# A decode layer on one core: three unused matmuls between the wide rows of w_down and the fold

## The chip, the cores and the metric

The kernel runs on one core of a Trainium2 chip. The metric is the device time of one execution in microseconds. Three runs of the kernel before took 409.50, 410.06 and 410.45 us; the median is 410.06. The engines are called TensorE (PE in the views, PEld for its weight loads), VectorE (DVE), ScalarE (ACT), GpSimd (POOL) and SyncE (SP, which issues the DMAs).

## What is computed

One token goes through a transformer layer with a cache of 65,536 positions. All inputs are bf16.

```python
def _A_ref(x, k_cache, v_cache, wq, wo):      # 32 query heads, 4 cache heads, head size 128
    q = (x @ wq).reshape(B, Sq, Hq, Dh).transpose(0, 2, 1, 3)
    k = jnp.repeat(k_cache, rep, axis=1)
    v = jnp.repeat(v_cache, rep, axis=1)
    p = _softmax(jnp.einsum("bhqd,bhkd->bhqk", q, k) * (Dh ** -0.5), axis=-1)
    o = jnp.einsum("bhqk,bhkd->bhqd", p, v)
    return o.transpose(0, 2, 1, 3).reshape(B, Sq, Hq * Dh) @ wo

def _B_ref(x, w_gate, w_up, w_down):          # 1024 -> 3584 -> 1024
    return (_gelu(x @ w_gate) * (x @ w_up)) @ w_down

h  = A_x + _A_ref(_layernorm(A_x), A_k_cache, A_v_cache, A_wq, A_wo)
h2 = h + _B_ref(_layernorm(h), B_w_gate, B_w_up, B_w_down)
```

## The kernel before

The two caches and the five weight matrices are read once, 173 MB in all, through one DMA queue that SyncE issues. A ring of four slots in SBUF takes wq, then the caches in eight turns (four cache heads, two halves each), then wo, w_gate, w_up and most of w_down. Because there is one token, every matmul has the weights or the cache as its moving operand. Its result is one useful row, and the kernel places four such narrow matmuls, 32 columns of the array each, side by side (`tile_position`).

The attention part is a list of operations with waits worked out by the class `Flow`, and a hardware loop of eight turns on TensorE (`pe_loop`). Its scores come from L464: 128x512 bf16 moving, 128x128 weights out of the tile `qs`. After the loop the tile `qs` and PSUM bank 5 are not used any more.

The feed-forward part is a plain program, in which TensorE's instructions stay in the order in which they are written (`manual_schedule`). w_down comes in four main loads, in this order: `wa` (4096 KB, the first 16 rows of each partition), `wb[:, 0:FM]` (2048 KB, 8 rows), `w_end[:, 0:3]` (768 KB, 3 rows) and the first five eighths of a last row (160 KB). The rest of that last row comes ahead of them in small pieces (L685 uses them). TensorE waits for each load on a semaphore of its own (`end_sem`).

The end of the kernel, in TensorE's order:

- L646 multiplies by w_up, L679 and L685 deal with the odd part of the last row.
- L665 (`down_wide`) multiplies the 16 rows of `wa`, two matmuls of 512 columns for each row, into bank 6 (`e_ps`), summing at four places of 32 partitions.
- L690 is ScalarE's copy of bank 6 to SBUF (`e_sb`), 128x512 f32.
- L671 (`add_wide`, the fold) adds the four places and brings them into the layout of the result: four f32 matmuls with the constant weights `fold`, two instructions each, into banks 2 and 7 (`d_ps`, `d_odd`).
- L657 (`down`) multiplies the other rows of w_down straight into those two banks, eight matmuls of 128 columns for each row: 64 for `wb`, 24 for the three rows in `w_end` and 5 for the last one, 93 in all.
- L699 and L700 cast the two banks to bf16, on VectorE and ScalarE, and L701 stores the result.

The fold reads what the copy writes, so TensorE waits for it between L665 and L671.

Of the kernel before, what the change touches and what calls it, by code (L numbers as in the profile page):

```python
# [118 lines left out]
def kernel(  # L119
# [13 lines left out]
    nc = tc.nc  # L133
    P = 128
# [21 lines left out]
    NB = 512  # L156
# [25 lines left out]
    def sb(name, shape, dtype=F32):  # L182
        return const.tile(shape, dtype, name=name)
# [3 lines left out]
    qs = sb("qs", [P, 4, NS, P + 1], BF16)  # L187
    sc = sb("sc", [P, CPH, NN, rep, NS])
    pt = sb("pt", [P, CPH, NN, rep, NS], BF16)
    bank = [psum.tile([P, NB], F32, name="bank%d" % i) for i in range(8)]  # L190
# [172 lines left out]
    for q in range(4):  # L363
        op("pe", "matmul", r=["q_bf"] + ["esel"], w=["B5"], out=qsel_ps[:, :, q, :], lhsT=esel[:, q, :], rhs=q_bf[:],
           start=True, stop=True)
# [156 lines left out]
    for dq in range(OQ):  # L522
        op("pe", "matmul", r=["o_sb", "osel"], w=["B4"], out=o2_ps, lhsT=osel[:, dq, :], rhs=o_sb[:, dq * Hq:(dq + 1) * Hq],
           start=(dq == 0), stop=(dq == OQ - 1))
# [17 lines left out]
    for c in range(Hq):  # L542
        for s in range(DS):
            q = 2 * (c % 2) + s
            op("pe", "matmul", r=["o2z", "R%d" % (2 + c // HC)], w=["B6"], out=at_ps[32 * q:32 * q + 32, :], lhsT=o2z[:, c, :],
               rhs=wv[:, c, :].rearrange("k (p s c) -> k s p c", s=DS, c=C4)[:, s], start=(c < 2), stop=(c >= Hq - 2), tile_position=(0, 32 * q))
# [104 lines left out]
    def down(a_row, w_row):  # L651
        blocks = w_row.shape[-1] // OB
        for j in (0, 4, 1, 5, 2, 6, 3, 7):
            if j >= blocks:
# [2 lines left out]
            nc.tensor.matmul((d_ps, d_odd)[q // 2][32 * q:32 * q + 32, :], lhsT=a_row[:, AZ - m:AZ - m + 32], rhs=w_row[:, j * OB:(j + 1) * OB],  # L657
                             start=False, stop=False, skip_group_check=True, tile_position=(0, 32 * q))

    e_sb = sb("e_sb", [P, NB])  # L660

    def down_wide(a_row, w_row, e):
        for h in range(DS):
            q = 2 * (e % 2) + h
            nc.tensor.matmul(e_ps[32 * q:32 * q + 32, :], lhsT=a_row[:, AZ:AZ + 32], rhs=w_row[:, h * NB:(h + 1) * NB],  # L665
                             start=False, stop=False, skip_group_check=True, tile_position=(0, 32 * q))

    def add_wide():
        for c in range(C4):
            h = c % 2  # L670
            nc.tensor.matmul((d_ps, d_odd)[h][64 * h:64 * h + 64, :], lhsT=fold[:, 1 - c // 2:65 - c // 2], rhs=e_sb[:, c * OB:(c + 1) * OB],  # L671
                             start=False, stop=False, skip_group_check=True, tile_position=(0, 64 * h))
# [9 lines left out]
    for s in range(GS + 1):  # L682
        q = 2 * (s % 2) + 1
        n = min(GN, P - s * GN)
# [3 lines left out]
    for e in range(FA):  # L688
        down_wide(actz[:, e, :], wa[:, e, :], e)
    nc.scalar.copy(out=e_sb[:], in_=e_ps[:])  # L690
    add_wide()
    e = FA
    for i, w_rows in ((2, wb[:, 0:FM, :]), (3, w_end[:, 0:FZ - 1, :]), (4, w_end[:, FZ - 1:FZ, 0:EC])):
# [38 lines left out]
```

## Time and profile before

| | |
|---|---|
| median of three runs | 410.06 us |
| the profiled execution: its time | 409.35 us |
| the profiled execution: its span, first to last instruction | 407.63 us |
| mean granted TensorE clock over the span | 0.803 |
| HBM read | 173.02 MB, 424 GB/s over the span |
| copy L690 | 400.57 to 401.16 us |
| fold L671 | 401.21 to 402.34 us |
| L657, 64 and 29 matmuls | 402.31 to 404.20 and 404.16 to 405.06 us |
| cast L699 | from 405.09 us |
| store L701 issued | 405.45 us |

Times inside the execution count from the first instruction of the span. A matmul's record goes from its start to a modelled end; matmuls overlap, so the distance between starts says how fast they follow one another. The granted clock is the share of full speed at which TensorE's array ran; in the records it is 1.0 or 0.5 and changes on a grid of 3.41 us, so a stretch with 0.59 is a mixture of the two. A DMA is complete when all its 16 parts have landed. "Idle before" is the time for which an engine had nothing running ahead of an instruction, with what ended it.

### The profile page before, as it was taken

What the parts mean: (1) busy time and instruction counts of PE and PEld (TensorE: products, weight loads), DVE (VectorE), ACT (ScalarE), POOL (GpSimd) and SP (SyncE); (2) the same over time, 40 slices, a digit from 0 to 9 for tenths busy, and PEclk for the clock granted to TensorE, in tenths of its full rate; (3) what the DMA queues carried; (4) which work ended last, traced back from release to release, by engine and by line L of the source; (5) the groups of instructions that cost most, each with busy time, mean ns of one, the idle gap of its engine ahead of it and who ended that gap; (6) DMA issues with size and microseconds to landing.
All of it is one profiled execution on the core that took longest, in us unless ns stands there. A gap on an engine that the chain in (4) does not pass through costs nothing. (4 is left out here: it accounts for less than half of the span.)

```text
span 407.6 us, 3801 instructions
## 1 busy us (share of the span) xinstructions
PE 226.5 (56%) x1546; PEld 99.3 (24%) x1546; DVE 201.4 (49%) x164; ACT 40.2 (10%) x143; POOL 14.6 (4%) x27
## 2 busy tenths in 40 slices
PE   0432854674677468716873686368456637634056
PEld 0110322231232133203321332133122213222023
DVE  4126860894079328734962686188509930111110
ACT  1000003000300130030003000300040022000000
POOL 4010000001000000010000001000000000001100
PEclk9995896899569778968896689589968986566686
DMA  8999999999999999999998999999999999999995
GB/s 360 412 453 420 447 428 412 460 419 431 434 460 418 412 441 479 418 408 415 495 424 386 441 421 453 415 463 412 412 460 460 418 408 424 457 450 424 405 410 222
DMA packets 5105, 173.10 MB, mean 425 GB/s; under 512 B 616, under 2 KB 876, under 8 KB 1004
## 3 DMA queue, kind: packets, MB, share of 16 engines
q1 hardware_dynamic: 5052, 173.02, 98.6%
q8 instruction: 4, 0.07, 0.1%
q10 hardware_dynamic: 48, 0.00, 0.0%
q14 instruction: 1, 0.01, 0.0%
HBM read 173.02 MB, written 0.00 MB: 424 GB/s over the span
## 5 line engine op out<-in xcount | busy, mean ns | idle before, releaser
L105 DVE STREAM_TRANSPOSE ktb<-ring 128x4096 f32<-128x4096 f32 x32 | 141.1, 4417 | 74.7 <-DMA ring<-in_A_k_cache_dram 74.7
L464 PE MATMUL bank<-ktb,qs 128*128 128x512 bf16 x512 | 130.0, 412 | 53.4 <-PEq L450 53.4
L464 PEld LDWEIGHTS bank<-ktb,qs 128*128 128x128 bf16 x512 | 50.9, 102 | 129.2 <-issue 82.1
L476 PE MATMUL bank<-ring,pt 128*32 128x512 bf16 x512 | 44.4, 522 | 38.0 <-PEq L450 38.0
L423 ACT ACTIVATE pt<-sc,nb 128x256 bf16<-128x256 f32 x64 | 31.5, 494 | 256.3 <-ACTq L419 256.3
L105 DVE STREAM_TRANSPOSE sc<-bank 128x512 f32<-128x512 f32 x32 | 22.2, 695 | 36.3 <-PE bank L464 36.3
L476 PEld LDWEIGHTS bank<-ring,pt 128*32 128x32 bf16 x512 | 18.5, 126 | 60.7 <-issue 56.7
L105 PE MATMUL bank<-ring,xz 128*32 128x512 bf16 (+1 forms) x128 | 11.9, 546 | 15.1 <-DMA ring<-in_B_w_gate_dram 8.2
L105 DVE TENSOR_REDUCE mx<-sc 128x8 f32<-128x2048 f32 x8 | 18.3, 2286 | 0.3
L468 PE MATMUL bank<-ident_f,mx 128*8 128x128 f32 x8 | 2.5, 308 | 25.8 <-PEq L450 25.8
L105 POOL COPY qs<-qsel 128x512 bf16<-128x512 bf16 x4 | 5.3, 1324 | 235.4 <-PE bank L464 219.8
L485 PE MATMUL bank<-sel,acc_sb 128*128 128x8 f32 x64 | 8.2, 255 | 6.9 <-PEq L450 6.9
L423 ACT ACTIVATION_READ_ACCUMULATOR pt<-sc,nb x64 | 12.0, 187 | 0.0
L485 PEld LDWEIGHTS bank<-sel,acc_sb 128*128 128x128 f32 x64 | 7.7, 191 | 10.7 <-issue 10.7
L646 PE MATMUL bank<-ring,xz 128*32 128x512 bf16 (+1 forms) x64 | 4.6, 457 | 9.3 <-PEq L641 9.3
L105 PEld LDWEIGHTS bank<-ring,xz 128*32 128x32 bf16 x128 | 4.4, 129 | 21.5 <-issue 12.7
L427 ACT COPY acc_sb<-bank 128x512 f32<-128x512 f32 x8 | 4.7, 585 | 47.9 <-ACTq L426 47.9
L623 DVE STREAM_TRANSPOSE ktb<-bank 128x512 f32<-128x512 f32 (+1 forms) x4 | 2.3, 618 | 13.3 <-PE bank L646 13.3
L105 PE MATMUL bank<-ring,ktb 128*32 128x512 bf16 x64 | 7.1, 618 | 1.7 <-DMA ring<-in_A_wo_dram 1.0
L468 PEld LDWEIGHTS bank<-ident_f,mx 128*8 128x8 f32 x8 | 0.7, 83 | 29.5 <-issue 29.5
L105 DVE STREAM_TRANSPOSE ktb<-bank 128x512 f32<-128x512 f32 x2 | 1.3, 694 | 12.6 <-PE bank L105 12.6
L470 PE MATMUL bank<-diag,ones_f 8*128 8x8 f32 x16 | 3.5, 286 | 5.7 <-PEq L450 5.7
(110 smaller groups left out, 65.7 us busy)
## 6 DMA issues: line engine op xcount, KB each, us to landing
ring<-in_A_k_cache_dram SPq DMA_DIRECT2D x16, 4096.0 KB, 24.8
ring<-in_A_wq_dram SPq DMA_DIRECT2D x2, 4096.0 KB, 16.6
ring<-in_A_wo_dram SPq DMA_DIRECT2D x2, 4096.0 KB, 25.4
ring<-in_B_w_gate_dram SPq DMA_DIRECT2D x1, 7168.0 KB, 24.6
ring<-in_B_w_up_dram SPq DMA_DIRECT2D x1, 7168.0 KB, 30.3
ring<-in_B_w_down_dram SPq DMA_DIRECT2D x1, 4096.0 KB, 17.5
ring<-in_B_w_down_dram SPq DMA_DIRECT2D x1, 2048.0 KB, 22.0
w_end<-in_B_w_down_dram SPq DMA_DIRECT2D x1, 768.0 KB, 23.4
```

The costliest lines, as they stand in the source:

```text
L105: ins = getattr(self.eng[e], o["call"])(**o["kw"])
L423: m = nc.scalar.activation(out=pt[:].rearrange("p c n h s -> p (c n) h s")[:, :, r, :], in_=sc[:].rearrange("p c n h s -> p (c n) h s")[:, ...
L427: nc.scalar.copy(out=acc_sb[:], in_=acc[:]).then_inc(from_act, 1)
L464: m = nc.tensor.matmul(bank[c][:], lhsT=qs[:, jt].rearrange("p s c -> p (s c)")[:, s * P:(s + 1) * P], rhs=mv[:, :, J, :, u], start=(s == ...
L468: nc.tensor.transpose(out=mxT_ps, in_=mx1[:], identity=ident_f).then_inc(s_step, 1)
L470: nc.tensor.matmul(bc_ps, lhsT=ones_f[0:rep, :], rhs=diag[:], start=True, stop=True).then_inc(s_step, 1)
L476: m = nc.tensor.matmul(acc[32 * q:32 * q + 32, :], lhsT=pt[:, c, n, :, :].rearrange("p h s -> p (h s)"), rhs=v_sb[:, c, :, n, :], start=(c ...
L485: m = nc.tensor.matmul(o_ps, lhsT=acc_sb[:, u * Dh:(u + 1) * Dh], rhs=sel[:, u:SQ:NS], start=(u == 0), stop=(u == NS - 1))
L623: nc.vector.transpose(out=r[:, o:o + n].rearrange("p (e j) -> p e j", j=32), in_=ps.rearrange("p (j e) -> p e j", j=32))
L646: nc.tensor.matmul(f_banks[t // 4][32 * q:32 * q + 32, :], lhsT=hz[:, ci, :], rhs=w, start=(ci == 0), stop=(ci == DC - 1), tile_position=( ...
```

## The change

Between the last wide row and the fold, three matmuls are issued. Each takes 128x128 bf16 weights and 128x512 bf16 moving data out of the old tile `qs` and writes bank 5, which nothing reads. They stand in TensorE's program behind L665 and ahead of the fold's wait for the copy, and wait for nothing of the feed-forward part. No other engine's instructions and no DMA are changed.

```diff
+    def stay_busy(n):
+        for i in range(n):
+            nc.tensor.matmul(bank[5][:], lhsT=qs[:, 0, 0, 0:P], rhs=qs[:, 1 + i % 3].rearrange("p s c -> p (s c)")[:, 0:NB], start=True, stop=True)
+
     e_sb = sb("e_sb", [P, NB])
...
     for e in range(FA):
         down_wide(actz[:, e, :], wa[:, e, :], e)
     nc.scalar.copy(out=e_sb[:], in_=e_ps[:])
+    stay_busy(3)
     add_wide()
```

## The prediction

> **What bounds the kernel now.** I read the page first, then the chain of waits, then the timeline of the last 12 us, then the DMA issues, and last the table by stages, cut on the grid of 3.41 us on which the granted clock changes. The page settles the whole: the DMA queue that carries the caches and weights is busy for 98.6% of the span, TensorE for 56%.
>
> ```profile
> PE 226.5 (56%) x1546; PEld 99.3 (24%) x1546; DVE 201.4 (49%) x164; ACT 40.2 (10%) x143; POOL 14.6 (4%) x27
> ...
> q1 hardware_dynamic: 5052, 173.02, 98.6%
> ```
>
> So only the stretch after the last big loads can give or take time. The chain of waits runs there through one transfer of w_down, the wide rows (L665), ScalarE's copy (L690), the fold (L671) and the rest of w_down (L657):
>
> ```profile
> 379.84 17.52 DMA ring<-in_B_w_down_dram
> 397.36 0.04 issue
> 397.40 3.15 PE bank L665 x32
> 400.55 0.02 issue
> 400.57 0.59 ACT e_sb L690
> 401.17 0.04 issue
> 401.21 1.12 PE bank L671 x8
> 402.34 2.77 PE bank L657 x63
> ```
>
> Read alone, it says that TensorE bounds the last 8 us and that everything queued there counts. The DMA list corrects that (columns: KB of one issue, us from issue to landing):
>
> ```profile
> ring<-in_B_w_down_dram SPq DMA_DIRECT2D x1, 2048.0 KB, 22.0
> w_end<-in_B_w_down_dram SPq DMA_DIRECT2D x1, 768.0 KB, 23.4
> w_end<-in_B_w_down_dram SPq DMA_DIRECT2D x1, 160.0 KB, 23.3
> ```
>
> With their issues just after 380.2, 380.7 and 381.2, these three land at 402.32, 404.17 and 404.57 (the last of their 16 landings in the trace). The first L657 matmul starts at 402.31: the fold's end and the landing fall together by chance. The 24 matmuls of the second load start at 404.16, again with the landing, after the first 64 had issued by 403.89. So from 402.3 on DMA sets two of three starts.
>
> The table by stages (PE busy, PEld, DVE, ACT, POOL, granted clock, DMA share, GB/s):
>
> ```profile
> 271.69:275.10 3.41, 3.41 (x9) 1.17 (x8) 3.41 (x1) 0.00 (x0) 0.00 (x0) 0.51 1.16 500
> 275.11:278.52 3.41, 3.41 (x17) 1.53 (x16) 2.31 (x3) 0.00 (x0) 0.00 (x0) 1.00 0.75 327
> ...
> 387.75:391.16 3.41, 2.87 (x32) 1.42 (x36) 0.00 (x0) 0.00 (x0) 0.00 (x0) 0.51 0.98 423
> 391.16:394.57 3.41, 1.71 (x36) 0.88 (x29) 1.64 (x4) 0.00 (x0) 0.00 (x0) 1.00 1.07 461
> 394.57:397.98 3.41, 1.89 (x24) 0.82 (x27) 0.19 (x1) 0.00 (x0) 0.00 (x0) 0.99 0.87 370
> 397.99:401.40 3.41, 2.73 (x30) 0.86 (x20) 0.00 (x0) 0.58 (x1) 0.00 (x0) 0.50 1.00 418
> 401.40:404.81 3.41, 3.41 (x99) 2.81 (x100) 0.00 (x0) 0.00 (x0) 0.00 (x0) 0.51 0.46 178
> ```
>
> Each stretch's clock follows TensorE's busy time in the stretch before it. 2.87 of 3.41 (84%) at 387.75 brought full clock at 391.16; 2.73 (80%) at 397.99 did not bring it at 401.40. Elsewhere in the span 2.79 sufficed (309.24, then 1.00) and 2.55 did not (350.20, then 0.51). The gap that keeps 397.99 to 401.40 at 80% is the 0.67 us in which TensorE waits for the copy.
>
> **The change part by part.** *Three matmuls added.* Their form, 128x512 bf16 on 128x128 weights, is that of L464, which fills the first two rows of the table: 8 weight loads in 3.41 us at half clock, 427 ns each, and 16 at full clock, 213 ns. The last four wide rows start at 399.88 to 399.90 and stream 427 ns, so the array is free at 400.31. The third filler is under way when the clock may rise at about 401.38: 400.31 + 2 x 0.427 = 401.16, 0.22 us at half clock (half of it), the other half in 0.11, free at 401.49. At half clock throughout: 400.31 + 1.28 = 401.59. The copy needs nothing of them (another bank) and ends at 401.16; the fold started at 401.21. So they delay the fold by 0.28 us, 0.38 at half clock, and by nothing (401.21 against 400.31 + 0.64) at full clock. Weight loads of 102 ns (L464) go beside the stream. There is no DMA, SP or POOL work in the edit. A wait for bank 5 or qs is long met: qs was last written at 253.7 us (POOL's fourth copy), bank 5 last read at 347.1 (the last o_raw copy). Behind them on TensorE stand the fold's 8 instructions and all 93 of L657.
>
> *Where the delay goes.* The fold's four pairs start 213 ns apart at half clock (401.48, 401.70, 401.91) and the array is free 0.81 us after its start. Delayed to 401.59 it is free at 402.40, under 0.1 us past the landing at 402.32; the 64 matmuls, 1.6 us, then stream till about 404.1, before 404.17. The two landings hide all of it; without them it would cost the whole 0.28 to 0.38.
>
> *The clock.* The fillers make the stretch to 401.40 busy nearly throughout, well over the 84% that sufficed. I take full clock from 401.4 to 404.8. The fold is then free no later than 402.30, still under the landing. L657's groups of four start 107 ns apart at half clock; the only full-clock pair of groups is the last one, 404.778 to 404.833, 55 ns. From 404.17: six groups take 0.33 us, streamed out at 404.50; then the landing at 404.57, five matmuls with the last start at about 404.64, and 0.22 us for one matmul (the 219 ns minimum at L657) end at 404.86. Before, the last ended at 405.06. Gain 0.20 us. The ends: if the narrow matmuls cannot come closer than 25 ns, the last start is 404.80 as before, and the gain 0; if the clock had risen only after the last matmul instead of at 404.8, before would have ended at 404.89 + 0.31 = 405.20, and the gain would be 0.34. I take 0.20, the row's own value: the 55 ns was measured on these matmuls.
>
> [...]
>
> *After the end.* Casts, the output's issue at 405.45 and its landing follow the last matmul at fixed distance. The sum: span 407.63 - 0.20 = 407.43. The profiled execution took 409.35, 1.72 outside its span, so 409.15; the median of the runs, 410.06, lies 0.71 above it and becomes 409.86.
>
> **Rivals.** *The clock gains nothing* (410.06, the last matmul at 405.06 as before): a gap as short as 0.67 us has no say in the clock, or the 3.41 us grid falls differently against the kernel in other runs, so that the tail has full clock already, or loses it again before the last rows. For it: the eight like turns over the cache have their half-clock stretches at different places. Against: a gap of 0.67 us leaves at most 80% of any stretch that holds it whole, and 80% did not raise the clock here. [...]
>
> *The landings do not bind in unprofiled runs* (faster). If w_down landed a microsecond sooner, TensorE would be the bound: before, the fold free at 402.02, 23 groups at 107 ns and 0.31 end at 404.8; after, fold from 401.49 free by 401.92 to 402.30, 23 x 0.0535 = 1.24 and 0.22 end at 403.4 to 403.8. That is 1.0 to 1.4 us less, 408.7 to 409.1. Against: 5 us from one landing to the next for 2 MB is the queue's 420 GB/s, the same as everywhere.
>
> *The copy is released only with the fillers* (slower). Place: L690, if its wait is met by a TensorE instruction behind the wide rows, or the fillers' writes hold up its read of PSUM. It would then start about 401.8 instead of 400.57, the fold about 402.45, a delay of 1.24 us; at half clock the last matmul ends at 402.45 + 0.81 + 23.25 x 0.107 + 0.2 = 405.95, 0.9 us late: 410.96. It decides only if the clock stays low: at full clock 402.45 + 0.43 + 0.86 = 403.74 is still ahead of the landing at 404.17, and nothing is lost. Against: before, the copy started 43 ns after the last wide row, with the fold and L657 already behind it in TensorE's program.
>
> **How the numbers follow.** Forecast 0.62 (409.86, given as 409.9); no gain 0.20; landings not binding 0.07; copy held or fillers on the path 0.11, about half of it over 0.8 us. 0.2% is 0.82 us, about what a measurement of this kernel can tell from no change; forecast and no-gain case both lie within it. With the runs' own spread (409.5 to 410.45) I put faster 0.09, same 0.82, slower 0.09. The forecast alone, with its ends of 0 to 0.34, is 409.7 to 410.1; the spread of the runs and part of the two outer rivals widen it to 409.3 to 410.6.
>
> **What would show it.** Granted clock 1.00 in the stretch from about 401.4; three matmuls of 128x512 between L665 and the fold; the fold's start 0.1 to 0.4 us behind the copy's end; L657's first start still at its landing, a wait of 0.5 us or more in front of the w_end rows, and the last matmul within 0.3 us of the last landing. Wrong if the copy starts later than 0.1 us after the wide rows, if L657's first start leaves its landing by over 0.2 us, or if the landings themselves move.

## The result and the profile after

The changed kernel takes 409.16 us (median of 19 runs, 409.09 to 409.55) against 410.06 (19 runs, 409.11 to 410.45). The ratio of the runs is 0.9985, 95% interval 0.9978 to 0.9992: about 0.6 us less, 0.3 to 0.9.

The runs say more than the medians. Of the 19 times before, 8 lie at 409.1 to 409.55 and 11 at 410.06 to 410.45, none between. Of the 19 after, all lie in the lower group. The change makes no good run better; it does away with the upper group. The execution profiled before, 409.35 us, was of the lower one. The gap between the groups is not always empty: of 62 further runs of the kernel before (those shared by the experiments below) 25 lie at 409.03 to 409.44, 22 at 409.90 to 410.41 and 15 between, at 409.52 to 409.77. What those 15 are no trace shows.

The end of the chain of waits after, up to the last cast (start, us, what):

```profile
382.19 22.10 DMA w_end<-in_B_w_down_dram
404.29 0.04 issue
404.33 0.74 PE bank L657 x29
```

The long TensorE chain from wide rows to last matmul is gone; a landing and the 29 matmuls behind it are what is left. Its timeline (start, us, engine, line, instruction; L669, L694, L675 are the wide rows, copy and fold in the changed file, L662 the unused matmuls):

```profile
397.95 3.27 PE L669 MATMUL bank<-ring,ktb 128*32 128x512 bf16 x32
...
401.16 0.82 PE L662 MATMUL bank<-qs 128*128 128x512 bf16 x3
401.28 0.58 ACT L694 COPY e_sb<-bank 128x512 f32<-128x512 f32 x1 [20.95 <-PE bank L669]
...
401.92 0.66 PE L675 MATMUL bank<-e_sb,fold 128*64 128x128 f32 x8
...
402.51 1.08 PE L657 MATMUL bank<-ring,ktb 128*32 128x128 bf16 x64
...
404.33 0.70 PE L657 MATMUL bank<-w_end,ktb 128*32 128x128 bf16 x29 [0.74 <-DMA w_end<-in_B_w_down_dram]
```

The unused matmuls run beside the copy; the fold starts 0.05 us behind the copy's end and takes 0.66 us instead of 1.12. L657's 64 matmuls take 1.08 instead of 1.90 us, and TensorE then waits 0.74 us for w_end. By the stages (PE busy, PEld, DVE, ACT, POOL, clock, DMA share, GB/s):

```profile
397.34:400.76 3.42, 3.42 (x33) 1.08 (x33) 0.00 (x0) 0.00 (x0) 0.00 (x0) 0.50 0.99 423
400.76:404.17 3.41, 2.83 (x83) 1.53 (x75) 0.00 (x0) 0.58 (x1) 0.00 (x0) 1.00 0.69 272
```

Read alone, this would mislead too. Here the grid fell so that wide rows filled 2.81 us of one stretch (397.95 to 400.76, 82%), and the clock rose at 400.76, before the first unused matmul (401.16). What the change does has to be seen in an execution of the upper group.

### The profile page after: what moved, and what is told of

It is laid out like the page before. It is cut to its first block, busy times and chain, and to the rows that moved or that the text cites. A ratio compares the mean times of both kernels' runs of the same rounds, so it can differ in the third digit from the quotient of the medians.

```text
span 407.6 us, 3807 instructions
## 1 busy us (share of the span) xinstructions
PE 229.8 (56%) x1549; PEld 100.0 (25%) x1549; DVE 201.5 (49%) x164; ACT 40.2 (10%) x143; POOL 14.6 (4%) x27
## 5 line engine op out<-in xcount | busy, mean ns | idle before, releaser
L464 PE MATMUL bank<-ktb,qs 128*128 128x512 bf16 x512 | 131.6, 416 | 51.1 <-PEq L450 51.1
L105 PE MATMUL bank<-ring,xz 128*32 128x512 bf16 (+1 forms) x128 | 13.3, 601 | 16.9 <-DMA ring<-in_B_w_gate_dram 10.1
L646 PE MATMUL bank<-ring,xz 128*32 128x512 bf16 (+1 forms) x64 | 5.9, 558 | 7.9 <-PEq L641 7.9
```

The lines of the kernel that those rows point to most:

```text
L105: ins = getattr(self.eng[e], o["call"])(**o["kw"])
L464: m = nc.tensor.matmul(bank[c][:], lhsT=qs[:, jt].rearrange("p s c -> p (s c)")[:, s * P:(s + 1) * P], rhs=mv[:, :, J, :, u], start=(s == ...
L646: nc.tensor.matmul(f_banks[t // 4][32 * q:32 * q + 32, :], lhsT=hz[:, ci, :], rhs=w, start=(ci == 0), stop=(ci == DC - 1), tile_position=( ...
```

## The experiments

The theory: the clock's grid falls differently in every execution, the upper group is a tail at half clock, and the unused matmuls end that half clock. Rivals: the six extra instructions (three loads, three matmuls) move the fetch of instruction blocks, and what they compute is irrelevant; or plain busy time counts, whatever the array does. Each kernel of the table ran ten times. "Upper" below counts times of 409.85 us and more.

| kernel | ratio to before, 95% | times, us | upper |
|---|---|---|---|
| e0: before, unchanged | 1.0005 (0.9995 to 1.0016) | 409.13 to 410.44 | 6 of 10 |
| e1: 4 columns each | 1.0011 (1.0001 to 1.0021) | 409.33 to 410.17 | 8 of 10 |
| e2: one unused matmul | 0.9992 (0.9983 to 1.0002) | 409.08 to 409.34 | 0 of 10 |
| e3: six | 1.0000 (0.9990 to 1.0011) | 409.01 to 410.28 | 3 of 10 |
| e6: before, two loads left out | 0.9989 (0.9972 to 1.0007) | 408.10 to 410.34 | 6 of 10 |
| e7: after, two loads left out | 0.9977 (0.9967 to 0.9987) | 408.19 to 409.31 | 0 of 10 |
| e8: fold moved | 1.0015 (1.0004 to 1.0027) | 409.10 to 410.90 | 7 of 10 |
| e9: 12 rows of the array | 1.0013 (1.0000 to 1.0026) | 409.13 to 410.80 | 6 of 10 |

Beside these, the kernel before gave 10 upper times of 31 in the runs shared by e0 to e3, and 12 of 31 in those shared by e6 to e9. With the first 11 of 19 and e0's 6 of 10 that is 39 of 91. How many fall into a sample moves the ratio of a kernel that is no different, so the groups are the better evidence.

The mean granted clock, on record for each execution of the experiments and of the changed kernel, says that the groups are no accident of the sample. Of 72 executions of the kernel before (the 62 and e0's 10), 25 have a mean of 0.787 or less, and 24 of these are upper. In e1, e8 and e9 16 executions have it, and all 16 are upper. With one or three unused matmuls 5 of 29 executions have it, and none is upper.

**e0, the kernel before once more.** No edit. 

> The kernel before, unchanged. Its 19 times lie in two groups, 409.1 to 409.6 us (8) and 410.05 to 410.45 us (11), with nothing between; the changed kernel's 19 all lie in 409.1 to 409.55. Clock theory: the two groups are two positions of the 3.41 us clock grid against the tail; a trace from the upper group has half clock from the wide rows to the last L657 matmul, which then ends about 0.35 to 1 us later after its landing. Code-fetch theory: a trace from the upper group has the 16 KB instruction packet (1.03 us) in the way of the last landings, so the w_end landing itself is later, whatever the clock. Both: ratio 1.000, both groups again.

The profiled execution was of the upper group: 410.44 us, span 408.7. Its timeline and its stages:

```profile
398.05 3.60 PE L665 MATMUL bank<-ring,ktb 128*32 128x512 bf16 x32
...
401.71 0.59 ACT L690 COPY e_sb<-bank 128x512 f32<-128x512 f32 x1 [21.94 <-PE bank L665]
...
402.35 1.12 PE L671 MATMUL bank<-e_sb,fold 128*64 128x128 f32 x8 [0.69 <-ACT e_sb L690]
...
403.40 1.90 PE L657 MATMUL bank<-ring,ktb 128*32 128x128 bf16 x64
405.08 1.06 PE L657 MATMUL bank<-w_end,ktb 128*32 128x128 bf16 x29
```

```profile
392.58:395.99 3.41, 1.38 (x28) 0.54 (x17) 1.83 (x5) 0.00 (x0) 0.00 (x0) 1.00 0.95 408
395.99:399.40 3.41, 3.37 (x27) 1.26 (x31) 0.00 (x0) 0.00 (x0) 0.00 (x0) 0.50 0.96 408
399.40:402.82 3.42, 2.73 (x28) 1.00 (x22) 0.00 (x0) 0.59 (x1) 0.00 (x0) 0.50 0.94 385
402.82:406.23 3.41, 3.33 (x101) 2.73 (x97) 0.05 (x1) 0.02 (x1) 0.00 (x0) 0.50 0.18 70
```

Half clock from 395.99 to 406.23. The wide rows take 3.60 us, the fold ends after wb's landing (402.62 in this trace), L657 starts 0.78 us behind that landing, and its 93 matmuls run without a wait to 406.15, 1.27 us behind the last landing (404.88). Nothing here is covered by DMA. The last landing is within 0.2 us of that in the trace after (404.69), and the 16 KB instruction packet starts at 401.6 to 401.8 in both, so a packet in the way of the landings is not the cause.

**e1, the same instructions with little work.**

```diff
-   matmul(bank[5][:], ..., rhs=...[:, 0:NB], ...)
+   matmul(bank[5][:, 0:4], ..., rhs=...[:, 0:4], ...)
```

> The three unused matmuls with 4 columns instead of 512: the same instructions, nearly no busy time. Clock theory: as the kernel before, ratio 1.000, both groups of times, half clock after 401.4 where the grid falls as in the trace before. Code-fetch theory: as the changed kernel, ratio 0.9985, no time over 409.7 us.

The upper group is back, 8 of 10. The rival of code fetch falls: the columns matter, not the instructions.

**e2, one instead of three.**

```diff
-    stay_busy(3)
+    stay_busy(1)
```

> One unused matmul instead of three. Clock theory: it covers 0.21 to 0.43 us of a 0.9 us pause of the array, so a stretch that holds the pause is 87% to 93% busy instead of 80%; 84% sufficed before, so the ratio is that of three, 0.9985; if the threshold stands higher, times of the upper group return. Code-fetch theory: two instructions moved instead of six, between 1.000 and 0.9985.

None of 10 is upper. At 39 of 91 the chance of that by luck is 0.57 to the tenth, 0.4%; at the 16 of 41 of the kernel before in the same rounds, 0.7%. The profiled execution has nearly the grid of e0's, 0.16 us earlier:

```profile
395.83:399.24 3.41, 3.37 (x27) 1.24 (x31) 0.00 (x0) 0.00 (x0) 0.00 (x0) 0.50 0.91 389
399.24:402.66 3.42, 2.73 (x28) 1.10 (x23) 0.00 (x0) 0.58 (x1) 0.00 (x0) 0.50 0.93 379
402.66:406.07 3.41, 2.10 (x101) 1.52 (x97) 0.28 (x1) 0.26 (x1) 0.00 (x0) 1.00 0.16 62
```

```profile
397.90 3.60 PE L669 MATMUL bank<-ring,ktb 128*32 128x512 bf16 x32
402.20 0.86 PE L675 MATMUL bank<-e_sb,fold 128*64 128x128 f32 x8 [0.69 <-ACT e_sb L694]
402.99 1.08 PE L657 MATMUL bank<-ring,ktb 128*32 128x128 bf16 x64
404.36 0.69 PE L657 MATMUL bank<-w_end,ktb 128*32 128x128 bf16 x29 [0.29 <-DMA w_end<-in_B_w_down_dram]
```

This pair is the cleanest reading of the change. Up to the copy the two are alike: wide rows at half clock, 3.60 us. Then one more matmul, and the next stretch has full clock: the 64 matmuls take 1.08 instead of 1.90 us, the last ends at 405.05 instead of 406.15, the span is 407.6 instead of 408.7. The unused matmul itself has no record in this trace, only its weight load at 401.43; the busy time of 2.73 us in both stretches therefore compares nothing. Counted by starts and streaming times (427 ns for 512 columns at half clock, the distance of the wide rows' groups in the trace before, 398.60 to 399.03), the array works from 399.40 to 401.45 and from 402.35 to 402.82 in e0, 2.5 of 3.41 us (74%), and without a rise; in e2 one matmul of 0.43 us more (an estimate by the same streaming time), 86%, and with one.

**e3, six.**

```diff
-    stay_busy(3)
+    stay_busy(6)
```

> Six unused matmuls. Both theories: the fold starts 0.64 us later than with three at full clock, 1.28 at half. Clock theory with the landings as cover: at full clock the 64 matmuls take 0.9 us and still end before the landing of w_end, so the time stays that of three, 0.9985 (at most 0.0005 more). If the end is TensorE's and the landings do not cover: 0.64 us or more on top, ratio 1.000 or above.

Seven of ten are as low as with three, though the fold starts 0.7 us behind the copy (402.48 against 401.79 in its trace): there the landing of w_end hides the delay. Three are upper, which was not expected. Six at half clock are 2.56 us in a pause of 0.9, more than the landings cover; that this is what the three runs show is only argued, since the profiled execution was a low one. By the count alone, 3 of 10 cannot be told from the 10 of 31 of the kernel before in the same rounds.

**e6 and e7, without the last landings.** Both leave out the loads of the last four rows of w_down (928 KB); L657 multiplies rows of wb in their place, so the matmuls stay.

```diff
-  (w_end[:, 0:FZ - 1, :], wb_src[:, FM:FB - 1, :], 3), (w_end[:, FZ - 1, 0:EC], last_row[:, 0:EC], 4)]
...
-  (3, w_end[:, 0:FZ - 1, :]), (4, w_end[:, FZ - 1:FZ, 0:EC])
+  (3, wb[:, 0:FZ - 1, :]), (4, wb[:, FZ - 1:FZ, 0:EC])
```

> The kernel before without the last two loads of w_down (928 KB): L657 multiplies rows of wb in place of the four rows of w_end, so the matmuls stay and two landings go. Landings-as-cover: where the tail runs at half clock TensorE, not DMA, sets the end, so the upper group of times stays within 0.2 us of where it is (409.9 to 410.4); the lower group gains at most 0.3 us (a tail from 402.3 that is at half clock ends at about 405.1). If landings bound both groups, all times fall by about 1 us or more.

> The changed kernel with the same two loads left out. Landings-as-cover: at full clock the last matmul ends 1.25 us of streaming and 0.22 us behind the fold's end (402.6 in the trace after), about 404.0 instead of 405.03: about 1 us less, 408.0 to 408.3. If TensorE bounded the changed kernel too, its time would stay near 409.16.

In e6 the upper group does not move at all (410.04 to 410.34) with its last two landings gone: TensorE bounds it. The lower group falls by a microsecond, to 408.10 to 408.30, against at most 0.3 expected. The expectation was read off the trace before, whose tail ran at half clock from 397.94 to 404.76; that the four lower runs of e6 had full clock there is argued, no trace of one is on record. In e7 the changed kernel spreads from 408.19 to 409.31; three of ten are within 0.05 us of what was expected, the others up to a microsecond above. The profiled execution, at 408.91, had half clock up to 402.37. So the clock seems still to differ between executions of the changed kernel, and the last landings level that out to the 409.09 to 409.55 of the result.

**e8, the fold behind the 64 matmuls.** No unused matmuls.

```diff
     nc.scalar.copy(out=e_sb[:], in_=e_ps[:])
-    add_wide()
...
             down(actz[:, e, :], w_rows[:, r, :])
             e += 1
+        if i == 2:
+            add_wide()
```

> No unused matmuls; the fold is moved behind L657's 64 matmuls on wb, so that TensorE waits for wb's landing instead of the copy, and the copy runs beside that. Clock theory: the pause is not gone, only bounded by another event (wide rows' end to wb's landing, 0.6 to 2 us), so half clock stays in many executions; but the fold, 0.8 us, is no longer between copy and landing. In the upper group L657 starts at wb's landing, 402.6, or when the wide rows end, instead of 403.40: 0.3 to 0.8 us less there, ratio 0.999 to 1.000, the two groups closer together. Rival (only the copy's wait counted): as the changed kernel, all times 409.1 to 409.5.

Seven of ten upper, and up to 410.90, higher than before. L657 did start at the landing in the profiled execution (402.35), but the fold moved past it:

```profile
402.35 1.90 PE L657 MATMUL bank<-ring,ktb 128*32 128x128 bf16 x64 [0.98 <-DMA ring<-in_B_w_down_dram]
...
404.18 1.12 PE L671 MATMUL bank<-e_sb,fold 128*64 128x128 f32 x8
```

```profile
402.64:406.05 3.41, 3.41 (x99) 2.83 (x89) 0.00 (x0) 0.00 (x0) 0.00 (x0) 0.50 0.16 64
```

The pause in front of L657 is 0.98 us instead of 0.69, it too is followed by half clock (the second view), and the fold now stands where no landing covers it. Exchanging the wait for the copy for the wait for a landing does not help; the gain of 0.3 to 0.8 us in the upper group did not come.

**e9, the same time on a tenth of the array.**

```diff
-   lhsT=qs[:, 0, 0, 0:P], rhs=qs[:, 1 + i % 3]...
+   lhsT=qs[0:12, 0, 0, 0:P], rhs=qs[0:12, 1 + i % 3]...
```

> The three unused matmuls read 12 partitions instead of 128: the same time on TensorE, a tenth of the array's rows. In the trace of the upper group a stretch filled by the odd row's matmuls (12 partitions) and wide rows, busy throughout in the records, did not bring full clock. If the clock goes by busy time: as the changed kernel, no time over 409.6. If it goes by how much of the array works: as the three small ones (e1), with the upper group back, ratio to before 1.000 or, since they delay the fold at half clock by 0.38 us, up to 1.001.

Six of ten upper, at 410.54 to 410.80, 0.6 us above e0's upper group by their medians (410.76 against 410.16). In the profiled execution the three matmuls over 12 partitions take 0.89 us of TensorE's time, against 0.82 for the three over 128 in the trace after; with them 6 of 10 runs are upper, as in e0 without any. (The profiled execution was a low one. In it the clock rose at 401.15, 0.18 us after the first of them had started, and the stretch before, from 397.74, had been filled by wide rows up to 400.83.) This is the slower outcome that the prediction had put down as "fillers on the path", 0.38 us there.

## Why the prediction was right, and where its size was off

The forecast was a small gain, 0.20 us, inside 0.2% of no change. By the ratio the gain is 0.6 us (0.3 to 0.9), three times that: 0.15%, with an interval that reaches 0.22%. Applied to the 410.06 us of the three runs on which the forecast stood, the ratio gives 409.44, inside the stated range of 409.3 to 410.6. The median of 409.16 is 0.14 below that range. How far a median moves hangs on how many of the runs before happen to be upper: in the later rounds the median of the kernel before was 409.56 and 409.57. That the forecast comes out as near as it does is in part luck. By its steps:

- *Each stretch's clock follows the one before it, and the 0.67 us pause is what holds it low.* Right in that the runs turned on the pause: 8 of 10 runs were upper with 4 columns (e1), none of 10 with one full matmul (e2). The yardstick was wrong: that 80% did not raise the clock and 84% did was read from busy time. The stretch 395.99 to 399.40 of e0 was busy for 3.37 of 3.41 us, more than half of it with matmuls over 12 partitions, and half clock followed; the like stretches of e2, e7 and e8 were busy for 3.34 to 3.41 us, and half clock followed in each. So a share of busy time does not say which clock follows. In e9 the same time over 12 partitions left 6 of 10 runs upper.
- *The landings hide the delay and cap the gain.* Right for the lower group, wrong for the upper. This is the step that set the size: that the landing bounds L657's first start was true of one execution, in which the wide rows had started at 397.40 and run partly at full clock. In e0 they start 0.65 us later, at half clock, and TensorE sets the end, 1.1 us behind the changed kernel's. The same mistake stands in the sum: it carried the 0.71 us by which the median lay above the profiled execution over unchanged. That is most of the distance between the groups, and it is what the change took away; after it the median, 409.16, lies no higher than the profiled execution, 409.31. The prediction had the mechanism as a rival, "the landings do not bind in unprofiled runs", 1.0 to 1.4 us, at 0.07. It held not because landings came earlier, as put there, but because TensorE came later, in 43% of the executions. 11 of the 19 executions, at some 1.0 us each, make the 0.6 us of the ratio; at 39 of 91 it would be 0.4.
- *The gap leaves the clock alone* (the rival). e0 and e2 speak against it: TensorE was idle for 0.69 us ahead of the fold in e0 and half clock followed from 402.82; with one matmul in that pause full clock followed from 402.66. That is a rise which fails to come, so neither says what makes the clock fall, and this stays open. In the trace before the clock fell at 397.94; between 392.87 and 397.40 there is, beside one matmul of 11 columns, only work over 12 or 8 partitions. It fell at 346.73 too, and TensorE's longest pauses about that are 0.87 and 1.27 us. The changes of clock lie multiples of 3.41 us apart in the traces before and after, and their places against the tail differ: 0.54 us behind the start of the wide rows before (397.94), 0.61 ahead of it after (397.34), 2.06 ahead in e0 (395.99). The prediction named the shifting grid only as a reason for no gain; it was the reason for a larger one.
- *Clock's effect on the rows.* Groups of four 55 ns apart at full clock were taken from a single pair; the trace after has 55 or 56 ns almost throughout, 14 ns a matmul, and 1.08 us for the 64. The 25 ns of the forecast's lower end is in the trace before the distance of the starts of the small matmuls on `x_in` (at 9.4 us); L657 came closer. The fold, bounded only, took 0.66 us.
- *Delay of the fold.* 0.28 us was forecast. It is 0.05 behind the copy in the trace after, whose unused matmuls ran at full clock (216 to 227 ns apart), and 0.05 with one (e2), both less than the 0.1 to 0.4 named as a sign. At half clock, where 0.38 was forecast, it is more: in e7's trace the fold starts 0.61 us behind the copy's end (402.50 against 401.89), and e9's upper runs lie 0.6 us above e0's.
- *Landings.* 402.32, 404.17 and 404.57 were each 0.05 us late in the prediction; from the first instruction of that trace they are 402.26, 404.12 and 404.52. No conclusion hangs on it. In the trace after, the last matmul ends 0.34 us behind the last landing, against the 0.3 named as a sign.
- *The copy held back.* It did not happen: copy 0.06 us behind the wide rows in the trace after.

## What to carry to other kernels

A median hides what a list of times shows: where the times fall into groups, one profile is a profile of one group, and a forecast needs a trace of each. In a tail that is shorter than a few periods of the clock's grid, look for the pauses that no DMA sets; one full-size matmul beside a copy (e2, none of ten runs upper) was worth more here than a new order of the same work (e8, seven of ten). Give such filler the least that does it: one was as good as three here, and with six three of ten runs were upper, for a reason that is only argued.

## What was not expected of the hardware

TensorE's busy time did not tell which clock followed. In e0 3.37 of 3.41 us were busy from 395.99, and half clock followed; in the trace after 3.42 of 3.42 from 397.34, and full clock followed. With three unused matmuls over 128 partitions none of 19 times was upper, with three of much the same length over 12 partitions (0.82 and 0.89 us in the profiled executions) 6 of 10 were, as in e0 without any. Streaming for 74% of a 3.41 us stretch was followed by half clock in e0; 82% (after, 397.95 to 400.76), 83% (L646 in the trace before, 388.29 to 391.11) and 86% (e2, an estimate) were followed by full clock.

The traces before and after have 92 whole stretches at half clock on record. Count in each the streaming time of the matmuls over 128 partitions, from their starts, their columns and the clock (f32 taken double, as the fold's pairs are 213 ns apart at half clock). In 39 stretches it came to 80% or more, and full clock followed each; in 53 to 74% or less, and half clock followed each. In e3 two stretches of the attention loop have 2.56 and 2.59 us of busy TensorE (75 and 76%), each here with the stretch after it (columns as in the views by stages):

```profile
66.23:69.64 3.41, 2.56 (x28) 1.10 (x32) 0.00 (x0) 0.56 (x3) 0.00 (x0) 0.50 1.07 461
69.65:73.06 3.41, 3.41 (x40) 1.43 (x36) 0.55 (x1) 0.00 (x0) 0.00 (x0) 0.50 1.03 442
182.28:185.69 3.41, 2.59 (x28) 1.16 (x32) 0.00 (x0) 0.48 (x2) 0.00 (x0) 0.50 1.03 442
185.70:189.11 3.41, 2.54 (x47) 1.28 (x39) 0.26 (x1) 0.58 (x1) 0.00 (x0) 1.00 0.96 413
```

Half clock followed the first, full clock the second. They lie 0.03 us apart, less than the 0.43 us of one matmul without a record, as e2's unused one is. What share is needed these runs do not show, nor whether rows or rows times columns count: wide rows on four strips of 32 columns came ahead of full clock (after, 397.95 to 400.76), and one strip alone was not tried.
